# Deferred roundings, pauses in attention, and an earlier first weight split in a one-core transformer block

## The chip, the cores and the metric

The kernel runs on one core of a Trainium2 chip. The metric is the device time of one execution in microseconds (us). TensorE (PE) does the matmuls and has a separate track for weight loads (PEld); VectorE (DVE), ScalarE (ACT) and GpSimd (POOL) do the rest, and SyncE (SP), ACT and POOL issue the transfers. Each engine works through its instructions in the order in which the program lists them.

## The reference, cut to what matters

The input x has 2048 rows of 576 features. It is normalised by row, and two branches work on the result: attention with 32 heads of width 18, in which each row sees 8 keys at distances 0, 2, ... 14, and a feed-forward layer of width 4608.

```python
xn = _layernorm(x, axis=-1)
return x + _A_ref(xn, A_wqkv, A_wo) + _B_ref(xn, B_w1, B_b1, B_w2, B_b2)
```

`_A_ref` multiplies xn with wqkv, gathers 8 keys and values for each row, takes a softmax over the 8 scores and multiplies the output with wo. `_B_ref` computes `relu(xn @ w1 + b1)**2 @ w2 + b2`.

## The kernel before

**Numbers in two parts.** A float32 operand is split into a rounded part ("hi", float32r) and a remainder ("lo"). ScalarE writes the hi with an ACTIVATE Copy, and VectorE then writes the lo as a subtraction (`tt`, L95), so every lo waits for the hi of ScalarE. A product is hi·hi + lo·hi + hi·lo on TensorE.

**Tiling and phases.** The rows are four blocks `b` of 512, taken in two pairs `s`. Two matmul stages (`ffn_pair` for x·W1 and `quad_step` for x·Wqkv) use a scheme of seven products in place of eight on a pair of blocks, which needs sums of x tiles (`sums`, `last_sum`; tiles SS and S4) and sums of weight tiles (slots T1 to T4 beside B11, B21, B22). The program runs through: rows of block 0 and q, k, v for the first pair (`q0`); `phase_a(0)`, 18 steps of W1 for blocks 0 and 1 with W2 for block 0; `phase_b0`, first 36 tiles of W2 for block 1 (L493 on TensorE, squared activations read back from DRAM as `h`), then q, k, v for the second pair in four half rounds of 14 `quad_step`s (L851, L855; weight halves k = 0, 1 and row halves), then the output projection of block 1; `phase_a(1)`; `phase_b1`.

**What fills the engines meanwhile.** `phase_b0` holds a list `pieces` of generators: `normalize(2)`, `normalize(3)`, `sums(1)`, `last_sum(1)`, and the first weight slots. After each W2 tile `run(pieces, 1 + n % 2)` advances them by one or two yields, and what is left of the count goes to `side`, which advances attention. Attention of one block and one of four head groups has 18 steps: four times a product of q with shifted keys and a reduction, the softmax (its exp is on ScalarE, L361), and four times a product with shifted values and a folding sum into `q`, after which POOL writes the result to DRAM in eight transfers (`o<-q`). `release` frees a buffer of keys or values (three of them, tile `kv`), and `fetch` then issues the next load on POOL's queue. Groups of block 1 come in the order 3, 2, 1, 0. `complete(b)` runs attention until nothing of block b is left, all of it at one place in the program; it is called for block 1 by the hook at `(k, half, s, i) = (0, 1, 6, 1)`, the end of the first two half rounds, followed by `regroup(1, 0)` and the loads for block 2, all on POOL.

**The quad rounds.** In each half round two row tiles i = 0, 1 go through s = 1, 2, 3, 5, 4, 7, 6. TensorE accumulates into PSUM banks a, b, c (names p_...). After s = 1 ScalarE copies a into b (L869), and s = 3 accumulates on b. After s = 4 the row of block 3 is b + c: ScalarE copies b into the staging tile `st` (L860) and VectorE adds c (`st<-p,st`). At s = 6 TensorE accumulates on c again, so that matmul waits until VectorE has read c.

**The order.** It is the order of the program: the kernel schedules all engines by hand, and an instruction that waits holds up everything behind it on its engine.

Of the kernel before, what the change touches and what calls it, by code (L numbers as in the profile page):

```python
# [8 lines left out]
F32 = mybir.dt.float32  # L9
# [19 lines left out]
QW = 3 * CG  # L29
# [16 lines left out]
def block_kernel(ctx: ExitStack, tc: tile.TileContext, x, xt, wqkv, wo, w1, b1, w2, b2, out):  # L46
# [47 lines left out]
    def tt(out, a, b, op):  # L94
        return nc.vector.tensor_tensor(out=out, in0=a, in1=b, op=op)  # L95
# [73 lines left out]
    def load_mb(b):  # L169
        assert b in measured  # L170
        mb[b] = sb.tile([P, 2, TB], F32, name="mb")
        nc.sync.dma_start(mb[b].rearrange("c k t -> c (k t)"), flat(mrscr[b], 0, [0, P], 2 * NJ * P))

    def normalize(b):
        open_x(b)
        for a in (0, 2):
            v = xm[b][:, a:a + 2]
            for k, op in enumerate((ALU.subtract, ALU.mult)):
                tt(v, v, mb[b][:, k:k + 1].to_broadcast([P, 2, TB]), op)
                if k:  # L180
                    nc.scalar.activation(X[b][:, 0, a:a + 2], v, AF.Copy)
# [20 lines left out]
    def sums(s):  # L202
        b0, b1 = 2 * s, 2 * s + 1
        hi = lambda a: X[b0][:, 0, a:a + 2].bitcast(F32)
        lo = lambda a: X[b0][:, 1, a:a + 2].bitcast(F32)
        f, v = xm[b1][:, :2], xm[b1][:, 2:]
        e = fourth_sum[s] = four()
        for i in (1, 2, 3):
            SS[i] = mt.tile([P, 2, 2, TB], F32R, name=f"S{i}")
        low = lambda i, a: tt(SS[i][:, 1], a, SS[i][:, 0].bitcast(F32), ALU.subtract)  # L210
        high = lambda i, a: nc.scalar.activation(SS[i][:, 0], a, AF.Copy)
        tt(v, f, v, ALU.add)
        high(1, v)
# [23 lines left out]
        left_hi(x4["d"], xf[b1])  # L237
        yield
        left_lo(x4["d"], xf[b1])
        yield  # L240

# [167 lines left out]

    def run(gens, k):  # L410

        while k > 0 and gens:
# [91 lines left out]
    def ffn_pair(s, p, work, first=False):  # L504
# [245 lines left out]
    def load_left(b):  # L750
        nc.sync.dma_start(xr[b][1][:D - DM], xt[b, :D - DM, NC - 1])
# [55 lines left out]
    def split_slot(name, v):  # L807
        split(*slot(name), v)
# [2 lines left out]
        t = ws[LEFT, f] = four(F32R)[:, :, :QW]  # L811
        split(t[:, 0], t[:, 1], raw[k, "left"][:, f])

    def first_slots(k):
        v, b12 = raw[k, 0][:, 0], raw[k, 0][:, 1]
        b21, b22 = raw[k, 1][:, 0], raw[k, 1][:, 1]
        if not k:
            split_slot(B11, v)
            yield
        tt(v, b12, v, ALU.subtract)  # L820
        yield
        split_slot(T1, v)
        yield
        tt(v, b22, v, ALU.subtract)
        yield
        split_slot(T2, v)
        yield
        tt(v, b21, v, ALU.subtract)
        yield

    def third_slot(k):
        v = raw[k, 0][:, 1]
        tt(v, raw[k, 1][:, 1], v, ALU.subtract)
        split_slot(T3, v)

    QKV_BANKS = [(2, 3, 4), (5, 6, 7)]
    rows_out = [0]
# [56 lines left out]
    def phase_b0():  # L894
        b = 1
        split_up.clear()
        pieces = [normalize(2), once(load_half, 0, 0), once(load_mb, 3), normalize(3), once(load_sides, 0), sums(1),
                  once(load_half, 0, 1), once(last_sum, 1), first_slots(0), once(third_slot, 0),
                  once(split_side, 0, 0), once(split_side, 0, 1)]
        open_y(b)  # L900
        for n in range(NF):
            w2_hi()
            if n % 2 == 0:
                h_hi(0, n // 2 + 1)
            add(b, tile_products(b, n, hs[0, n // 2]), range(NC) if n == NF - 1 else ())
            w2_lo()
            if n % 2 == 0:
                h_lo(0, n // 2 + 1)
            if n % 2 and n // 2 + 3 < NP:
                load_h(0, n // 2 + 3)  # L910
            run(pieces, 1 + n % 2)
            if n == 3:
                load_xt(3)
            if n == 31:
                run_all(pieces)
            if n == 33:
                residual(b)
                xr[b].append(sb.tile([P, TB], F32, name="xf"))
                load_left(b)
            if n == 34:  # L920
                split_slot(B21, raw[0, 1][:, 0])
        for c in range(NC):
            drain(b, c)
            if c in (1, 3):
# [7 lines left out]
        def hook(k, half, s, i):  # L932
# [9 lines left out]
            if half and not k:  # L942
                if (s, i) == (1, 1):
                    split_slot(B11, raw[1, 0][:, 0])
                if (s, i) == (3, 1):
                    slots = first_slots(1)
                    for _ in slots:
                        pass
                if (s, i) == (5, 1):
                    split_slot(B21, raw[1, 1][:, 0])  # L950
                if (s, i) == (4, 1):
                    third_slot(1)
                if (s, i) == (7, 1):
                    fourth_slot(1)
                    split_side(1, 0)
                if (s, i) == (6, 1):
                    split_side(1, 1)
                    split_slot(B22, raw[1, 1][:, 1])
# [304 lines left out]
    def q0():  # L1263
# [21 lines left out]
        for r in range(len(todo) - 2):  # L1285
# [23 lines left out]
            if r == 21:  # L1309
# [86 lines left out]
```

## Time and profile before

| | |
|---|---|
| times of three runs | 1144.18, 1145.52, 1146.80 us; median 1145.52 |
| the profiled execution's own time, its span | 1146.9 us, 1145.2 us |
| PE busy | 1113.7 us, 97% |
| DVE busy | 936.2 us, 82% |
| ACT busy | 586.9 us, 51% |
| POOL busy | 116.9 us, 10% |
| mean granted TensorE clock | 0.99 |

A group's row gives the line, engine, operation, output and inputs, shapes and count, then busy time and mean ns of one, then the idle time of the engine just before it and what ended it. In a timeline the first number is the start from the span's beginning, the second the length, and the bracket holds the idle time before. In windows the engine columns are busy us with the number of instructions; PEclk is the granted clock. TensorE is busy nearly always, so what a change does is read from where it is not: the first W1 step near 96 us, the W2 tiles of `phase_b0` between 439 and 577 us, and the start of the quad rounds near 580 us.

### The profile page before, as it was taken

How to read it: one execution, taken by the hardware profiler on the slowest of the kernel's cores; microseconds unless marked ns; L12 is line 12 of the kernel's file. 1: busy time of each engine (PE TensorE's matmuls, PEld its weight loads, DVE VectorE, ACT ScalarE, POOL GpSimd, SP SyncE). 2: the span in 40 equal slices, each digit the busy share in tenths (PEclk: the TensorE clock that was granted, in tenths of full speed). 3: DMA queues.
4: the chain of work that ended last, by engine and by line, in shares of the span. 5: the costliest groups of instructions: out<-in, count | busy, mean ns of one | idle time of the engine just before them, and what ended most of it. 6: DMA issues, size and time to landing. Idle time of an engine off the chain costs nothing.

```text
span 1145.2 us, 13847 instructions
## 1 busy us (share of the span) xinstructions
PE 1113.7 (97%) x4966; PEld 932.8 (81%) x4966; DVE 936.2 (82%) x1238; ACT 586.9 (51%) x823; POOL 116.9 (10%) x219
## 2 busy tenths in 40 slices
PE   9998999999999999797989999999999999999998
PEld 7997888878888888576879988888888888888887
DVE  7696998989888987587986669898989888889864
ACT  5334665656556654335325436665566565533441
POOL 4000210202102020000102000110102020201100
PEclk9999999999999999899989999999999999999999
DMA  8953655393936376555566764635545463765672
GB/s 287 335 177 113 210 182 180 103 245 125 231 120 223 135 283 204 200 181 185 167 219 224 221 223 135 220 125 201 175 144 176 147 209 106 262 220 185 217 260 88
DMA packets 89557, 218.86 MB, mean 191 GB/s; under 512 B 12040, under 2 KB 40464, under 8 KB 83984
## 3 DMA queue, kind: packets, MB, share of 16 engines
q1 hardware_dynamic: 59456, 154.85, 40.4%
q0 software_dynamic: 10544, 52.14, 14.2%
q10 hardware_dynamic: 19488, 10.99, 3.2%
q8 instruction: 39, 0.64, 0.2%
q14 instruction: 30, 0.25, 0.1%
HBM read 174.21 MB, written 43.73 MB: 190 GB/s over the span
## 4 chain that ended last, share of the span: by engine, by line
PE 76%; DVE 13%; DMA 4%; issue 3%; ACT 3%; POOL 0%; SPq 0%; ACTq 0%; DVEq 0%; POOLq 0%
PE p L493 35%; PE p L524 26%; PE p L851 6%; PE p L528 5%; DVE pr L95 3%; DVE w1r L95 2%; DMA w2r<-in_w 2%; PE p L304 1%; DVE h L95 1%; DVE w2s L95 1%; PE p L855 1%; DVE w1s L95 1%; PE p L1180 1%; DVE lg L353 1%; DMA kvq<-st 1%
## 5 line engine op out<-in xcount | busy, mean ns | idle before, releaser
L493 PE MATMUL p<-h,w2s 128*128 128x512 f32 x2066 | 500.7, 393 | 16.0 <-ACT h L779 7.8
L493 PEld LDWEIGHTS p<-h,w2s 128*128 128x128 f32 x2066 | 389.6, 189 | 104.4 <-ACT h L779 10.3
L524 PE MATMUL p<-X,w1s 128*128 128x512 f32 x864 | 220.7, 391 | 4.5 <-DVE w1s L95 3.1
L524 PEld LDWEIGHTS p<-X,w1s 128*128 128x128 f32 x864 | 162.5, 188 | 39.3 <-DVE w1s L95 3.5
L466 ACT ACTIVATE w2s<-w2r 128x640 fp32r<-128x640 f32 x164 | 119.6, 733 | 112.4 <-PE p L493 91.3
L524 PE MATMUL p<-S,w1s 128*128 128x512 f32 x648 | 164.8, 390 | 0.0
L95 DVE TENSOR_TENSOR w2s<-w2r,w2s 128x576 fp32r<-128x576 f32 x164 | 123.5, 753 | 46.9 <-ACT w2s L466 46.5
L524 PEld LDWEIGHTS p<-S,w1s 128*128 128x128 f32 x648 | 121.9, 188 | 25.5
L381 POOL DMA_DIRECT2D o<-q x128 | 69.4, 607 | 703.1 <-DVE q L95 701.2
L95 DVE TENSOR_TENSOR w1s<-w1r,w1s 128x1024 fp32r<-128x1024 f32 (+1 forms) x78 | 94.2, 1209 | 27.0 <-ACT w1s L439 20.1
L531 ACT ACTIVATE r<-r,b1t 128x512 f32<-128x512 f32 x72 | 52.0, 723 | 111.8 <-DVE r L95 111.5
L95 DVE TENSOR_TENSOR pr<-q,kv 128x1152 f32<-128x1152 f32 x64 | 86.8, 1356 | 1.5
L95 DVE TENSOR_TENSOR pr<-lg,kv 128x1152 f32<-128x1152 f32 x64 | 86.6, 1353 | 0.8
L353 DVE TENSOR_REDUCE lg<-pr 128x64 f32<-128x1152 f32 x64 | 86.4, 1350 | 0.9
L95 DVE TENSOR_TENSOR pr<-pr 128x576 f32<-128x576 f32 (+1 forms) x128 | 77.6, 606 | 3.4
L439 ACT ACTIVATE w1s<-w1r 128x1024 fp32r<-128x1024 f32 x72 | 75.7, 1052 | 2.7 <-PE p L851 1.8
L95 DVE TENSOR_TENSOR h<-r,h 128x1024 fp32r<-128x1024 f32 (+3 forms) x46 | 51.8, 1137 | 30.8 <-ACT r L539 23.4
L539 ACT ACTIVATE r<-r 128x1024 f32<-128x1024 f32 x72 | 75.4, 1050 | 0.1
L95 DVE TENSOR_TENSOR w1r<-w1r 128x256 f32<-128x256 f32 (+3 forms) x118 | 66.1, 560 | 4.6 <-DMA w1r<-in_wqkv 2.0
L528 PE MATMUL p<-x,w1s 128*128 128x512 f32 x216 | 66.5, 389 | 0.0
L95 DVE TENSOR_TENSOR r<-p,r 128x512 f32<-128x512 f32 (+1 forms) x77 | 52.8, 686 | 9.6 <-ACT r L589 6.0
L568 ACT ACTIVATE r<-p 128x512 f32<-128x512 f32 x36 | 21.6, 600 | 68.7 <-PE p L524 68.7
(169 smaller groups left out, 1111.7 us busy)
## 6 DMA issues: line engine op xcount, KB each, us to landing
w2r<-in_w SPq DMA_DIRECT2D x144, 320.0 KB, 3.1
kv<-kvq POOLq DMA_DIRECT2D x29, 1296.0 KB, 7.0
w1r<-in_w SPq DMA_DIRECT2D x36, 640.0 KB, 4.9
h<-r SPq DMA_DIRECT2D x36, 512.0 KB, 3.3
h<-h SPq DMA_DIRECT2D x36, 512.0 KB, 4.1
kvq<-st ACTq DMA_DIRECT2D x48, 216.0 KB, 2.8
w2r<-in_wo SPq DMA_DIRECT2D x20, 320.0 KB, 3.0
w1r<-in_xt SPq DMA_DIRECT2D x6, 1024.0 KB, 6.8
```

What stands on the lines that cost most here:

```text
L95: return nc.vector.tensor_tensor(out=out, in0=a, in1=b, op=op)
L353: nc.vector.tensor_reduce(out=lg[:, j * HG:(j + 1) * HG].rearrange("p a w -> p w a"), in_=pr.rearrange("p w (a d) -> p w a d", d=DH), axis ...
L381: nc.gpsimd.dma_start(rows[:, i], q[i * L:(i + 1) * L, :, a:z])
L439: nc.scalar.activation(w1s[n, k][:, 0], raw1[n][:, 4 * k:4 * k + 4], AF.Copy)
L466: nc.scalar.activation(w2s[stream[i]][:, :DE], raw2[i], AF.Copy)
L493: nc.tensor.matmul(yp[b][c], v, a, start=c not in yb[b], stop=c in last and c not in [o[0] for o in ops[i + 1:]], skip_group_check=True)
L524: nc.tensor.matmul(to, l, r, start=start and i == 0, stop=i == len(mm) - 1, skip_group_check=True)
L528: nc.tensor.matmul(to, weight(LEFT, k, f), v, start=False, stop=k == 1, skip_group_check=True)
L531: nc.scalar.activation(to, a, AF.Relu, bias=b1t[:, f:f + 1])
L539: nc.scalar.activation(r, r, AF.Square)
L568: nc.scalar.activation(u[:, 0], bb, AF.Copy)
L851: nc.tensor.matmul(to, l[:, js], r, start=start and n == 0, stop=n == len(mm) - 1, skip_group_check=True)
```

## The change

1. `soon(f)` and `flush()`: with `defer[0]` set, a hi is put in a list in place of being issued; it is issued at the next `flush()`, which stands at the start of every `run()` and ahead of a lo. `defer` is set for the part of `phase_b0` up to n = 33.
2. In `phase_b0` the pieces have rests in them (`rest(4)` between the two normalisations, `rest(2)` ahead of the slots; each yield makes one attention step), the transfer of block 3's mean and scale (`load_mb(3)`) goes ahead of `load_half`, `last_sum` and the slots are cut into more yields (hi in one, lo in a later one), and T3 and the side slots are now in the same generator. `run` stops at n < 33, and what is left runs at n = 33 in place of 31.
3. The slots of the second weight half are spread over the second half round: hi at one hook, lo at a later one.
4. In `ffn_pair` the attention steps for s = 0 go from 3 to `2 + p % 2`.
5. In `q0` the first W1 tile is split at rows 23 and 24 in place of 24 and 25, and row 22 runs no piece.

```diff
+    later, defer = [], [False]
+    def soon(f):
+        if defer[0]:
+            later.append(f)
+        else:
+            f()
+    def flush():
+        while later:
+            later.pop(0)()
...
     def normalize(b):
...
-                    nc.scalar.activation(X[b][:, 0, a:a + 2], v, AF.Copy)
+                    soon(lambda v=v, a=a: nc.scalar.activation(X[b][:, 0, a:a + 2], v, AF.Copy))
...
-        left_hi(x4[b], xf[b])
+        soon(lambda: left_hi(x4[b], xf[b]))
         yield
         for a in (0, 2):
+            flush()
             tt(X[b][:, 1, a:a + 2], xm[b][:, a:a + 2], X[b][:, 0, a:a + 2].bitcast(F32), ALU.subtract)
...
     def sums(s):
...
-        low = lambda i, a: tt(SS[i][:, 1], a, SS[i][:, 0].bitcast(F32), ALU.subtract)
-        high = lambda i, a: nc.scalar.activation(SS[i][:, 0], a, AF.Copy)
+        def low(i, a):
+            flush()
+            tt(SS[i][:, 1], a, SS[i][:, 0].bitcast(F32), ALU.subtract)
+        high = lambda i, a: soon(lambda: nc.scalar.activation(SS[i][:, 0], a, AF.Copy))
...
     def run(gens, k):
+        flush()
...
     def ffn_pair(s, p, work, first=False):
...
-            side(1 if p == 1 else 2 + p % 2 if s else 3, False)
+            side(1 if p == 1 else 2 + p % 2, False)
...
+    def rest(k):
+        for _ in range(k):
+            side(1)
             yield
...
     def phase_b0():
...
-        pieces = [normalize(2), once(load_half, 0, 0), once(load_mb, 3), normalize(3), once(load_sides, 0), sums(1),
-                  once(load_half, 0, 1), once(last_sum, 1), first_slots(0), once(third_slot, 0),
-                  once(split_side, 0, 0), once(split_side, 0, 1)]
+        defer[0] = True
+        pieces = [normalize(2), once(load_mb, 3), once(load_half, 0, 0), rest(4), normalize(3), once(load_sides, 0),
+                  sums(1), once(load_half, 0, 1), last_sum_parts(1), rest(2), first_slots()]
...
-            run(pieces, 1 + n % 2)
+            if n < 33:
+                run(pieces, 1 + n % 2)
...
-            if n == 31:
+            if n == 33:
                 run_all(pieces)
-            if n == 33:
+                defer[0] = False
                 residual(b)
...
             if half and not k:
                 if (s, i) == (1, 1):
-                    split_slot(B11, raw[1, 0][:, 0])
+                    slot(B11)
+                    slot_hi(B11, v)
+                if (s, i) == (2, 0):
+                    slot_lo(B11, v)
...
-            if r in (24, 25):
-                w1_hi(0, r - 24)
-                w1_lo(0, r - 24)
-            elif r != 3:
+            if r in (23, 24):
+                w1_hi(0, r - 23)
+                w1_lo(0, r - 23)
+            elif r not in (3, 22):
                 run(pieces, 3 if r < 1 or 15 <= r < 20 else 1 if r > 20 else 2)
```

TensorE's order is the same in both programs, and no engine has more or fewer instructions in all. What moves is on VectorE and ScalarE, at three places.

**VectorE at the end of the first two half rounds** (k = 0), where `complete(1)` stands. Bank c of row tile 0 is p_4658 before and p_4592 in the change. Before:

```order
L95 TENSOR_TENSOR r_4967<-mb,r_4967 128x432
L95 TENSOR_TENSOR st<-p_4670,st 128x432
L95 TENSOR_TENSOR r_4981<-mb,r_4981 128x432
L95 TENSOR_TENSOR h<-w1r,h 128x2x432
L95 TENSOR_TENSOR pr<-q,kv 128x1152
L353 TENSOR_REDUCE lg<-pr 128x8x8
L95 TENSOR_TENSOR pr<-q,kv 128x1152
L353 TENSOR_REDUCE lg<-pr 128x8x8
L95 TENSOR_TENSOR st<-p_4658,st 128x432
```

In the change, from the same weight slot (B22's lo, `h<-w1r,h`) on:

```order
L95 TENSOR_TENSOR r_4911<-mb,r_4911 128x432
L95 TENSOR_TENSOR h<-w1r,h 128x2x432
L95 TENSOR_TENSOR pr<-pr 128x576
L95 TENSOR_TENSOR pr<-pr 128x288
L95 TENSOR_TENSOR q<-pr 128x144
L95 TENSOR_TENSOR pr<-lg,kv 128x1152
```

and, with 32 rows between, its end:

```order
L95 TENSOR_TENSOR pr<-lg,kv 128x1152
L95 TENSOR_TENSOR pr<-pr 128x576
L95 TENSOR_TENSOR pr<-pr 128x288
L95 TENSOR_TENSOR q<-pr 128x144
L95 TENSOR_TENSOR pr<-q,kv 128x1152
L372 TENSOR_REDUCE lg<-pr 128x8x8
L95 TENSOR_TENSOR pr<-q,kv 128x1152
L372 TENSOR_REDUCE lg<-pr 128x8x8
L95 TENSOR_TENSOR st<-p_4592,st 128x432
```

Before, block 2's first attention steps follow the slot at once. In the change 40 rows of block 1's attention stand between them: the last three folding sums of group 1 with the two value products between them, and all of group 0 (four query products and reductions, the softmax, four value products and folding sums).

**ScalarE at the same place**, from B22's hi on (L869 is L920 in the change, L874 is L925, L361 is L380). Before:

```order
L99 ACTIVATE r_4981<-mb 128x432
L99 ACTIVATE h<-w1r 128x2x432
L869 ACTIVATE p_4657<-p_4656 128x432
L869 ACTIVATE p_4668<-p_4667 128x432
L874 ACTIVATE p_4659<-p_4657 128x432
```

In the change:

```order
L99 ACTIVATE r_4911<-mb 128x432
L99 ACTIVATE h<-w1r 128x2x432
L380 ACTIVATE lg<-lg 128x256
L920 ACTIVATE p_4591<-p_4590 128x432
L920 ACTIVATE p_4602<-p_4601 128x432
L925 ACTIVATE p_4593<-p_4591 128x432
```

The exp of group 0 now stands ahead of the copies of a into b for the next half round.

**ScalarE in the first W2 tiles of `phase_b0`**, with the hi of block 2's x (X, L181 before, L193 in the change; `w2s<-w2r` is the hi of a W2 tile, L466 and L486). Before:

```order
L466 ACTIVATE w2s<-w2r 128x640
L181 ACTIVATE X_3768<-w1r 128x1024
L466 ACTIVATE w2s<-w2r 128x640
L779 ACTIVATE h<-h 128x1024
L181 ACTIVATE X_3768<-w1r 128x1024
L466 ACTIVATE w2s<-w2r 128x640
L195 ACTIVATE x_3769<-xf 128x512
```

In the change:

```order
L486 ACTIVATE w2s<-w2r 128x640 x2
L799 ACTIVATE h<-h 128x1024
L193 ACTIVATE X_3724<-w1r 128x1024
L486 ACTIVATE w2s<-w2r 128x640
L193 ACTIVATE X_3724<-w1r 128x1024
L209 ACTIVATE x_3725<-xf 128x512
```

A hi of x now stands behind the hi of the next W2 tile, where it stood ahead of it.

More of the change, by code (lines that the diff above doesn't have):

```diff
@@ L410, in run @@
     def run(gens, k):
+        flush()
         while k > 0 and gens:
@@ L812, in split_side, with slot_hi, slot_lo, last_sum_parts @@
         split(t[:, 0], t[:, 1], raw[k, "left"][:, f])
[L814 to L818, printed above, removed]
+    def slot_hi(name, v):
+        soon(lambda: nc.scalar.activation(ws[name][0], v, AF.Copy))
+    def slot_lo(name, v):
+        flush()
+        tt(ws[name][1], v, ws[name][0].bitcast(F32), ALU.subtract)
+    def rest(k):
+        for _ in range(k):
+            side(1)
             yield
-        tt(v, b12, v, ALU.subtract)
+    def last_sum_parts(s):
+        b, e = 2 * s + 1, fourth_sum[s]
+        soon(lambda: nc.scalar.activation(X[b][:, 0, :2], e, AF.Copy))
         yield
-        split_slot(T1, v)
+        flush()
+        tt(X[b][:, 1, :2], e, X[b][:, 0, :2].bitcast(F32), ALU.subtract)
+        yield
+    def first_slots():
+        v, w, b21, b22 = raw[0, 0][:, 0], raw[0, 0][:, 1], raw[0, 1][:, 0], raw[0, 1][:, 1]
+        for name in (B11, T1, T2, T3):
+            slot(name)
+        slot_hi(B11, v)
+        yield
+        slot_lo(B11, v)
+        yield
+        tt(v, w, v, ALU.subtract)
+        slot_hi(T1, v)
+        yield
+        tt(w, b22, w, ALU.subtract)
+        slot_hi(T3, w)
+        yield
+        slot_lo(T1, v)
         yield
         tt(v, b22, v, ALU.subtract)
+        slot_hi(T2, v)
         yield
-        split_slot(T2, v)
+        slot_lo(T3, w)
+        yield
+        slot_lo(T2, v)
         yield
         tt(v, b21, v, ALU.subtract)
+        for f in range(2):
+            ws[LEFT, f] = four(F32R)[:, :, :QW]
+            soon(lambda f=f: nc.scalar.activation(ws[LEFT, f][:, 0], raw[0, "left"][:, f], AF.Copy))
         yield
[L831 to L834, printed above, removed]
+        for f in range(2):
+            flush()
+            tt(ws[LEFT, f][:, 1], raw[0, "left"][:, f], ws[LEFT, f][:, 0].bitcast(F32), ALU.subtract)
+            yield
     QKV_BANKS = [(2, 3, 4), (5, 6, 7)]
@@ L919, in phase_b0 @@
                 load_left(b)
+                slot(B21)
+                slot_hi(B21, raw[0, 1][:, 0])
             if n == 34:
-                split_slot(B21, raw[0, 1][:, 0])
+                slot_lo(B21, raw[0, 1][:, 0])
         for c in range(NC):
@@ L957, in hook @@
                     split_side(1, 1)
-                    split_slot(B22, raw[1, 1][:, 1])
+                    split_slot(B22, b22)
                     complete(1)
```

31 lines of the change are left out of this document (25 added, 6 removed).

## The prediction

> **What bounds the kernel now.** I read the page first, then TensorE's waits, then the windows and timelines around them.
>
> ```profile
> PE 76%; DVE 13%; DMA 4%; issue 3%; ACT 3%; POOL 0%; SPq 0%; ACTq 0%; DVEq 0%; POOLq 0%
> ```
>
> TensorE is the bound (the chain that ended last is three quarters PE), and its work does not change. So the change can win only what TensorE now waits, and lose what it will wait. TensorE's waits by engine and line (total, times, longest, us):
>
> ```profile
> PE p L493 <- ACT h L779: 7.8, 6, 3.1
> PE p L493 <- DVE w2s L95: 5.8, 1, 5.8
> PE p L851 <- DVE h L759: 4.9, 1, 4.9
> PE p L524 <- DVE w1s L95: 3.1, 1, 3.1
> ```
>
> The first two are the W2 tiles of `phase_b0`, the third the first quad rounds, the last the first W1 step. The whole of the W2 stage (504 matmuls, 439 to 577 us) stands in one group: its idle time is 15.7 us. A long wait also lowers the granted clock behind it (window: PE busy and count; then the other engines; then the clock):
>
> ```profile
> L493 PE MATMUL p<-h,w2s 128*128 128x512 f32 x504 | 122.1, 402 | 15.7 <-ACT h L779 7.8 <-DVE w2s L95 5.8 <-ACT w2s L466 2.0
> 470.00:480.00 10.00, 7.82 (x22) 6.22 (x23) 7.29 (x7) 2.35 (x3) 0.00 (x0) 0.66 0.32 97
> 540.00:550.00 10.00, 6.85 (x24) 5.32 (x23) 9.31 (x16) 4.93 (x7) 0.00 (x0) 0.83 0.33 109
> 560.00:570.00 10.00, 10.00 (x46) 8.27 (x45) 9.86 (x12) 3.29 (x4) 4.35 (x8) 1.00 0.61 182
> 580.00:590.00 10.00, 6.95 (x25) 6.51 (x26) 8.67 (x14) 2.18 (x4) 0.00 (x0) 0.66 0.53 167
> 630.00:640.00 10.00, 10.00 (x53) 9.60 (x52) 8.64 (x9) 3.18 (x6) 0.54 (x1) 1.00 1.03 337
> ```
>
> At full clock 10 us hold 46 W2 matmuls or 53 quad matmuls. So 22 in 7.82 us of busy time lost 7.82 − 4.78 = 3.0 us, 24 in 6.85 lost 1.6, and 25 in 6.95 lost 2.2: a mean of 2.3 us for each wait of 3 to 6 us.
>
> **The change, part by part: what it wins.** In the W2 stage the big wait has a transfer behind it, and the small ones a rounding ahead of a W2 tile's:
>
> ```profile
> 470.23 1.23 DVE L95 TENSOR_TENSOR w1r<-w1r,mb 128x1024 f32<-128x1024 f32 x1 [7.71 <-DMA mb<-mr]
> 474.43 1.06 ACT L181 ACTIVATE X<-w1r 128x1024 fp32r<-128x1024 f32 x1 [13.49 <-DVE w1r L95]
> 476.14 0.76 DVE L95 TENSOR_TENSOR w2s<-w2r,w2s 128x576 fp32r<-128x576 f32 x1 [1.75 <-ACT w2s L466]
> ```
>
> VectorE waited 7.71 us for block 3's mean and scale. Four rests put its use about three tiles later, 3 · 14 / 4.6 = 9.1 us, and the transfer is issued ahead of two others: this wait goes. The last rows show the ping-pong: the remainder of the W2 tile waits 1.75 us since ScalarE rounds x first, which itself waits for VectorE. With x rounded behind the next W2 tile that goes too. What can be won is 15.7 + 3.0 + 1.6 = 20.3 us. Against it: in the first 21 tiles VectorE has, by these durations, 21 · 0.76 of W2 remainders, 11 · 1.22 of `h`, and 38 us of normalisation, sums and rests (22 operations of 1.22, 8 of half that width, by estimate 0.7 each, and rests of two value products with their sums, 6.0), 67 us together, where TensorE needs 21 · 3.04 = 64. So it runs level with TensorE, and something may still be late: I leave 2 us (bounds 0 and 12) and count 18.3. Behind it VectorE has room, since attention has left this stage: in the 560 to 570 window it was 99% busy and TensorE ran through.
>
> At the start of the quad rounds TensorE waited 4.92 us for the drains of the finished banks, which stood behind attention on VectorE; now two rows of W2 stand there. I count 4.9 + 2.2 − 0.5 = 6.6 us (bounds 4 and 7).
>
> In the first W1 step TensorE waited 3.1 us for the first remainder:
>
> ```profile
> 89.24 1.60 DVE L95 TENSOR_TENSOR w1r<-w1r 128x512 f32<-128x512 f32 x3
> 95.29 2.35 DVE L95 TENSOR_TENSOR w1s<-w1r,w1s 128x1024 fp32r<-128x1024 f32 x2
> ```
>
> One value product and its folding sum (3.0 us below) leave the way, and the hi is issued a row sooner, right behind the combination that ends at 90.84: the win is 2.9 us (bounds 2 and 4). The fewer steps in `phase_a(0)` cost nothing there, since TensorE does not wait in it; what they put off is counted next. Together 18.3 + 6.6 + 2.9 = 27.8 us.
>
> **What it loses.** Attention steps are not saved but put off: 8 in `phase_a(0)` (one for each even p from 2 to 16), 1 in `q0`, and by the counts of yields about 12 in the W2 stage. What is left falls due at `complete(1)`, as 40 VectorE rows in one piece. Their prices, from the same steps elsewhere in this stage:
>
> ```profile
> 579.59 0.41 DVE L359 TENSOR_REDUCE mx<-lg 128x32 f32<-128x256 f32 x1
> ...
> 582.25 2.73 DVE L759 SCALAR_TENSOR_TENSOR h<-p,b2t,h 128x512 f32<-128x512 f32 x4
> ...
> 587.97 1.35 DVE L95 TENSOR_TENSOR pr<-lg,kv 128x1152 f32<-128x1152 f32 x1
> 589.35 1.25 DVE L95 TENSOR_TENSOR pr<-pr 128x576 f32<-128x576 f32 x2
> 590.64 0.31 DVE L95 TENSOR_TENSOR q<-pr 128x144 f32<-128x144 f32 x1
> 590.98 1.36 DVE L95 TENSOR_TENSOR pr<-lg,kv 128x1152 f32<-128x1152 f32 x1
> ...
> 604.75 0.31 DVE L95 TENSOR_TENSOR q<-pr 128x144 f32<-128x144 f32 x1
> ...
> 627.92 1.05 DVE L95 TENSOR_TENSOR h<-w1r,h 128x864 fp32r<-128x864 f32 x1
> 628.89 1.35 DVE L95 TENSOR_TENSOR pr<-q,kv 128x1152 f32<-128x1152 f32 x1
> ...
> 631.67 1.36 DVE L95 TENSOR_TENSOR pr<-q,kv 128x1152 f32<-128x1152 f32 x1
> ...
> 634.39 0.61 DVE L95 TENSOR_TENSOR st<-p,st 128x432 f32<-128x432 f32 x1
> ```
>
> A value product with its sum takes 590.98 − 587.97 = 3.01 us, the sum alone 1.6, a query product with its reduction 631.67 − 628.89 = 2.78, the softmax 582.25 − 579.59 = 2.66. The piece is 1.6 + 2 · 3.01 + 4 · 2.78 + 2.66 + 4 · 3.01 = 33.4 us. On the clock of before it starts at 628.97, where B22's remainder ends, and ends at 662.4.
>
> Behind it stand four steps of block 2's attention, which need a new load of keys. POOL issues that load only after the result of the last group and its regrouping:
>
> ```profile
> 605.35 4.32 POOL L381 DMA_DIRECT2D o<-q  x8 [38.77 <-DVE q L95]
> 609.72 0.56 POOL L693 DMA_DIRECT2D kv<-o  x1
> 611.46 0.54 POOL L693 DMA_DIRECT2D kv<-o  x1 [1.18 <-DMA o<-q]
> 619.99 0.54 POOL L324 DMA_DIRECT2D q<-kvq  x1 [7.99 <-DMA kvq<-st]
> kv<-kvq POOLq DMA_DIRECT2D x29, 1296.0 KB, 7.0
> 638.30 1.32 PE L851 MATMUL p<-h,X 128*128 128x432 f32 x6
> ```
>
> Before, this queue ran at 605, with over 20 us to spare. From the last `q` (604.75 + 0.31) to the end of the regrouping's issue (612.00) are 6.9 us; the queries' issue is 0.5, the keys land 7.0 after theirs: 14.4 us. So the keys are there at 662.4 + 14.4 = 676.8. Then come the four steps, 634.39 − 628.89 = 5.5, and `st<-p` for bank c, 0.6: 682.9. TensorE wants bank c at 638.30 (its s = 6). It waits 44.6 us, of which about 21 pass earlier, at s = 3: the exp stands ahead of the copies on ScalarE and cannot start before 628.97 + 7.6 + 11.1 + 0.9 = 648.6. That part is inside the 44.6, not added. With 2.3 us of low clock after it, the loss is 46.9 us. Bounds: 30.2 + 2.3 if the keys did not hold (the 33.4 alone, 668.5 − 638.30), and 49 if the load takes 2 us more. I take the long chain, since each step of it has its row. Two low-clock spells cost no more than one, as the first lies in the second wait.
>
> The Trainium skill (TensorE: Matmul & The Clock Gate, section "What's actually happening") says that TensorE falls to half clock after an idle window of about 3.4 us and comes back after a busy one of the same length. By that the restart would cost an estimated 1.7 us and the loss 46.3; the windows above, with 0.66 after 5.8 and 4.9 us and 1.00 around the waits of 1 us, agree in kind. The Trainium skill (DMA: Bandwidth & Descriptors, section "Anatomy of one DMA — SWDGE (gpsimd) path") prices a transfer at 2.0 us plus its bytes at 436 GB/s, an estimated 5.0 us for the keys, which would make the loss 2 us smaller; the row of 7.0 is from this kernel with other traffic beside it.
>
> **The sum.** 46.9 − 27.8 = +19.1 us, on the span of 1145.2 gives 1164.3. The profiled execution took 1146.9, so 1166.0 like it; against the median of 1145.5 the same step gives 1164.6.
>
> **The rivals.** *VectorE stays the bound in the W2 stage*: the 67 against 64 us bring new small waits, and only 8 of 20.3 us are won. For it: VectorE level with TensorE. Against: at 99% busy it held TensorE up nowhere. 1164.6 + 10 = 1175. *The keys come in time*, so that only the 33.4 us count: −14.4, 1150. It needs POOL free of the last group's result, which its order speaks against. *The piece is hidden and the kernel is faster*: TensorE would have to find bank c read less than 25.5 us late (27.8 − 2.3), so the keys in time and 5 of the 33.4 us done before B22's remainder. With this and nothing left at c it ends at 1143, and at 1118 if nothing waited. Against: the piece has one place in the program, and no engine steps over a waiting row. *The deferral does nothing*: the roundings wait elsewhere, only 9.5 us are won, and the time is 1145.5 + 46.9 − 9.5 = 1183. Against: ScalarE is half idle, and the order shows each hi behind the W2 tile's.
>
> **How the numbers follow.** Forecast 0.68, VectorE bound 0.13, keys in time 0.08, hidden 0.05, deferral idle 0.06. The forecast's own bounds are 1157 to 1174. I widen to 1149 and 1178, which takes in the second and third and leaves out the last two and some of the tails. A change under 0.2%, 2.3 us, cannot be told from none here. Faster: 0.06, the hidden case and a tail. Same: 0.03. Slower: 0.91.
>
> **What would show it.** Right: between 439 and 577 TensorE's idle time falls from 15.7 to a few us and the clock stays at 1.00; the wait at L851 on the drain is gone; there are two new waits at the quad matmuls, some 20 us on ScalarE's copies of a into b and then over 20 us on `st`, in the third half round; VectorE has a run of over 30 us of attention without a gap, then a gap of about 14 us that a transfer of keys ends. Wrong: no such gap (keys in time), or the W2 stage still idle by 10 us. The likeliest error of size is the wait for the keys, 14.4 us, and the 2 us left in the W2 stage.

## The result, and the profile after

The changed kernel takes 1156.49 us (median; 1156.03 to 1157.82), the kernel before 1145.15 us beside it: a ratio of 1.0099, 95% interval 1.0082 to 1.0117. It is slower, by 11 us where 19 were forecast. The profiled spans are 1156.1 and 1145.2 us.

Line numbers shift: L493, L524, L466, L851, L860, L869, L759 and L779 of before are L513, L544, L486, L902, L911, L920, L779 and L799 after. The chain of work that ended last, by engine, and TensorE's waits (total, times, longest, us), of the changed kernel:

```profile
PE 91%; DVE 5%; DMA 1%; issue 1%; ACT 1%; POOL 0%; ACTq 0%; POOLq 0%; DVEq 0%
...
PE p L902 <- DVE st L95: 23.6, 1, 23.6
PE p L902 <- ACT p L920: 19.9, 1, 19.9
...
PE p L544 <- DVE w1s L95: 0.4, 1, 0.4
PE p L513 <- ACT h L555: 0.2, 1, 0.2
```

The waits of before in the W2 tiles and at the drains are gone, and the one in the first W1 step is down from 3.1 to 0.4 us. Two new ones have come, in the third half round. TensorE's timeline of the changed kernel (start, length, operation, and in the bracket the idle time before it):

```profile
433.10 114.70 PE L513 MATMUL p<-h,w2s 128*128 128x512 f32 x504
547.64 2.51 PE L902 MATMUL p<-r,X 128*128 128x432 f32 x12
...
567.22 2.48 PE L902 MATMUL p<-r,X 128*128 128x432 f32 x12
...
586.76 2.48 PE L902 MATMUL p<-r,X 128*128 128x432 f32 x12
589.08 2.50 PE L902 MATMUL p<-w1s,S 128*128 128x432 f32 x12
611.48 3.91 PE L902 MATMUL p<-w1s,S 128*128 128x432 f32 x12 [19.89 <-ACT p L920]
...
646.81 2.53 PE L902 MATMUL p<-h,X 128*128 128x432 f32 x6 [23.59 <-DVE st L95]
...
653.94 2.48 PE L902 MATMUL p<-r,X 128*128 128x432 f32 x12
```

The 504 products of the W2 stage stand in one unbroken row of 114.70 us, where before they were 122.1 us with 15.7 us of idle time. The third half round starts at 586.76 and ends at 653.94. On VectorE, ScalarE and POOL of the changed kernel stands why:

```profile
590.88 1.25 DVE L95 TENSOR_TENSOR pr<-pr 128x576 f32<-128x576 f32 x2
...
624.08 0.31 DVE L95 TENSOR_TENSOR q<-pr 128x144 f32<-128x144 f32 x1
640.71 1.36 DVE L95 TENSOR_TENSOR pr<-q,kv 128x1152 f32<-128x1152 f32 x1 [16.32 <-DMA kv<-kvq]
...
646.16 0.60 DVE L95 TENSOR_TENSOR st<-p,st 128x432 f32<-128x432 f32 x1
```

```profile
610.59 0.42 ACT L380 ACTIVATE lg<-lg 128x256 f32<-128x256 f32 x1 [21.10 <-DVE lg L95]
610.91 0.93 ACT L920 ACTIVATE p<-p 128x432 f32<-128x432 f32 x2
```

```profile
624.68 4.31 POOL L400 DMA_DIRECT2D o<-q  x8 [21.54 <-DVE q L95]
...
631.84 0.54 POOL L345 DMA_DIRECT2D kv<-kvq  x1
```

The piece of attention runs on VectorE from 590.88 to 624.39 without a gap, 33.5 us. The exp inside it stands ahead of ScalarE's copies of a into b (L920): TensorE's first wait ends with them. VectorE then stands for 16.32 us before keys that POOL could issue only behind the last `q`. Four steps later comes the `st<-p` row that TensorE's second wait is for.

By stages, from the starts of TensorE's rows in both timelines (us):

| stage | before | after | gain | forecast |
|---|---|---|---|---|
| up to the first W2 product (first W1 step) | 117.71 | 113.72 | 4.0 | 2.9 |
| `phase_a(0)`, to the W2 stage of block 1 | 321.4 | 319.4 | 2.0 | 0 |
| W2 stage, 504 products | 137.7 | 114.5 | 23.1 | 18.3 |
| first half round (drains ahead of it) | 26.8 | 19.6 | 7.2 | 6.6 |
| second half round | 19.6 | 19.5 | 0.1 | 0 |
| third half round | 19.7 | 67.2 | −47.4 | −46.9 |
| fourth half round, and the rest | 502.2 | 502.2 | 0 | 0 |

The gains sum to 36.4 us, the loss is 47.4: 11.0 us, which is the difference of the spans, 10.9.

### The profile page after: what moved, and what is told of

Its sections match the earlier page's. It is cut to its first block, busy times and chain, and to the rows that moved or that the text cites. A ratio compares the mean times of both kernels' runs of the same rounds, so it can differ in the third digit from the quotient of the medians.

```text
span 1156.1 us, 13845 instructions
## 1 busy us (share of the span) xinstructions
PE 1105.7 (96%) x4966; PEld 931.0 (81%) x4966; DVE 938.3 (81%) x1238; ACT 588.2 (51%) x823; POOL 117.5 (10%) x219
## 4 chain that ended last, share of the span: by engine, by line
PE 91%; DVE 5%; DMA 1%; issue 1%; ACT 1%; POOL 0%; ACTq 0%; POOLq 0%; DVEq 0%
PE p L513 45%; PE p L544 29%; PE p L548 5%; PE p L323 5%; PE p L902 5%; DVE pr L95 2%; PE p L1253 1%; PE p L906 1%; DMA kv<-kvq 1%; DVE lg L372 1%; DMA kv<-in_x 0%; DVE w1s L95 0%; POOL o L400 0%; DVE r L95 0%; PE p L1215 0%
## 5 line engine op out<-in xcount | busy, mean ns | idle before, releaser
L513 PE MATMUL p<-h,w2s 128*128 128x512 f32 x2066 | 493.2, 390 | 0.3 <-ACT h L555 0.2
L513 PEld LDWEIGHTS p<-h,w2s 128*128 128x128 f32 x2066 | 387.2, 188 | 83.6 <-ACT h L555 1.0
L544 PE MATMUL p<-X,w1s 128*128 128x512 f32 x864 | 219.5, 389 | 0.4 <-DVE w1s L95 0.4
L544 PEld LDWEIGHTS p<-X,w1s 128*128 128x128 f32 x864 | 162.1, 188 | 34.3 <-DVE w1s L95 0.8
L486 ACT ACTIVATE w2s<-w2r 128x640 fp32r<-128x640 f32 x164 | 120.5, 735 | 128.4 <-PE p L513 97.9
L544 PE MATMUL p<-S,w1s 128*128 128x512 f32 x648 | 164.5, 389 | 0.0
L544 PEld LDWEIGHTS p<-S,w1s 128*128 128x128 f32 x648 | 121.6, 188 | 25.3
L95 DVE TENSOR_TENSOR pr<-q,kv 128x1152 f32<-128x1152 f32 x64 | 86.8, 1357 | 17.9 <-DMA kv<-kvq 16.3
L588 ACT ACTIVATE r<-p 128x512 f32<-128x512 f32 x36 | 21.6, 599 | 71.2 <-PE p L544 71.2
```

The lines of the kernel that those rows point to most:

```text
L486: nc.scalar.activation(w2s[stream[i]][:, :DE], raw2[i], AF.Copy)
L513: nc.tensor.matmul(yp[b][c], v, a, start=c not in yb[b], stop=c in last and c not in [o[0] for o in ops[i + 1:]], skip_group_check=True)
L544: nc.tensor.matmul(to, l, r, start=start and i == 0, stop=i == len(mm) - 1, skip_group_check=True)
```

## The experiments

All edits are on the changed kernel, but for e; the diffs of g and l are shown against f and k. Ratios are to the kernel before, run beside it, with 95% intervals.

**a: the number of attention steps in `phase_a(0)` put back.**

```diff
-            side(1 if p == 1 else 2 + p % 2, False)
+            side(1 if p == 1 else 2 + p % 2 if s else 3, False)
```

> The change with its fourth edit undone (three attention steps for s = 0 again). Theory (the loss is the attention that falls due in one piece at complete(1), and the keys' load queued behind it): the piece shrinks to the end of the softmax and four value products, 1.2 + 4 * 3.01 = 13.3 us in place of 33.4, and the exp leaves it, so the wait of 19.9 us on ScalarE's copies goes and the wait on st is the key chain alone; phase_a(0) is 2 us longer. 1156.5 - 20.1 + 2.0 = 1138.4. Rival (the length of the piece does not decide, the keys or the order on ScalarE do): 1150 or more. Rival (the steps taken out of phase_a(0) are what gave the 6 us there): phase_a(0) 6 us longer, 1142.

Measured: 1137.91 us, 0.9936 [0.9915, 0.9958]. The piece has shrunk to the softmax's tail and four value products, 13.3 us, the wait on L920 is gone, and the third half round takes 46.4 us in place of 67.2. So the piece's length sets a part of the loss one to one: 20.1 us less piece, 20.8 us less time. `phase_a(0)` itself takes 320.7 us here, 1.3 us more than in the changed kernel.

**b: no deferral.**

```diff
-        defer[0] = True
+        defer[0] = False
```

> The change with the roundings issued at once (the list is never used), all rests and the earlier transfer kept. Theory (the deferral removes the small waits, the rests and the earlier transfer the one long wait): the W2 stage gets back the waits on ScalarE of before, 9.9 us idle and some 2 us of low clock, 114.5 to about 126 us, and the loss at the quad rounds stays: 1166 to 1169. Rival (the rests and the lighter load of attention won the whole stage, the deferral nothing): 1156.5.

Measured: 1165.49 us, 1.0176 [1.016, 1.0191]. The group of W2 products in b, in the window of its stage:

```profile
L513 PE MATMUL p<-h,w2s 128*128 128x512 f32 x504 | 117.1, 392 | 5.0 <-ACT h L799 4.2 <-ACT w2s L486 0.6
```

The waits on ScalarE are back: 5.0 us idle and 117.1 − 114.7 = 2.4 us more of busy time, 7.4 together, where some 12 were expected. The rival "the deferral does nothing" falls. But the deferral is a third of the 23.1 us; the other two thirds come from what else the change did to this stage.

**c: no attention steps in the third half round.**

```diff
-                    if (s, i) in (...) and (k, half) != (0, 1):
+                    if (s, i) in (...) and (k, half) not in ((0, 1), (1, 0)):
```

> The change without the attention steps of the third half round, so that the bank's read no longer stands behind steps that need the new keys. Theory: the wait for the keys (16.3 us) and the four steps (5.4 us) leave the way, the piece of 33.4 us stays, with the wait of 19.9 us on ScalarE: 1156.5 - 21.5 = 1135, up to 1138 if the keys hold the fourth half round. Rival (the piece on VectorE alone sets the end of the wait, the keys arrive within it): no change, 1156.5. Rival (the eight steps put off come back as a new piece in phase_a(1)): 1146 or more.

Measured: 1144.86 us, 0.9991 [0.9982, 1.0001], some 10 us above what was expected. The third half round did what it should: 43.0 us in place of 67.2, so the keys' wait and the four steps behind it are 24.2 us of the loss. But the fourth takes 25.3 us in place of 19.5, and the rest 489.2 in place of 482.6. In the fourth it is the keys again, as VectorE's timeline of c shows: the wait for them has moved there and is shorter.

```profile
641.83 1.36 DVE L95 TENSOR_TENSOR pr<-q,kv 128x1152 f32<-128x1152 f32 x1 [8.99 <-DMA kv<-kvq]
```

That the longer rest is the steps that were left out, coming back later, is argued here and not shown. The rival "come back as a new piece" had 1146 or more, and the time lies between the two.

**d: a and c together.**

> Both: three steps for s = 0 and no attention in the third half round. Theory: the piece of 13.3 us ends about 2 us after TensorE wants the bank, and the keys hold the fourth half round for about 3 us, so of the 47.4 us some 5 are left, and phase_a(0) is 2 us longer: 1156.5 - 47.4 + 7 = 1116. Rival (the two parts overlap and only one of them can be had): 1135. Rival (steps put off cost it later): 1125 or more.

Measured: 1126.54 us, 0.9833 [0.9818, 0.9849], again some 10 us above: the time is that of the rival "steps put off cost it later" (1125 or more). TensorE's and VectorE's timelines of d:

```profile
587.06 2.48 PE L902 MATMUL p<-r,X 128*128 128x432 f32 x12
...
605.29 1.69 PE L902 MATMUL p<-h,X 128*128 128x432 f32 x6 [3.23 <-DVE st L95]
...
611.65 2.48 PE L902 MATMUL p<-r,X 128*128 128x432 f32 x12
```

```profile
621.40 1.36 DVE L95 TENSOR_TENSOR pr<-q,kv 128x1152 f32<-128x1152 f32 x1 [6.86 <-DMA kv<-kvq]
```

The third half round takes 24.6 us. So the loss comes apart into two parts that nearly add: with the long piece 67.2 us with the keys' wait and 43.0 without it, with the short one 46.4 and 24.6. The keys cost 24.2 or 21.8 us, the 20 us of piece 20.8 or 18.4. What stays open in d is 4.9 us here (the 13.3 us of piece), 3.4 in the fourth half round, where VectorE still stands for keys at 621.40, and 6.2 in the rest.

**e: the earlier W1 split alone, on the kernel before.**

```diff
-            if r in (24, 25):
+            if r in (23, 24):
...
-            elif r != 3:
+            elif r not in (3, 22):
```

> The kernel before with only the last part of the change: the first W1 tile is split at rows 23 and 24 instead of 24 and 25, and row 22 issues no pieces. My theory takes the first W1 step as a term by itself: the changed kernel starts the first W2 product at 113.72 us against 117.71 us, so 4.0 us should come through to the end and nothing else should move: 1141 us (1140 to 1142). A rival says that the step only hands its wait on, because the W2 stage of block 1 is bound by VectorE and the later stages have slack of their own: then the first W2 product starts sooner and the end stays at 1145 us.

Measured: 1142.06 us, 0.9952 [0.9939, 0.9964]; the span is 3.8 us shorter. The first W2 product starts at 113.69, 4.0 us sooner. The win comes through; it is not handed on.

**f: the piece laid out over the third half round.** `complete(1)`, `regroup` and the offers move from the hook (0, 1, 6, 1) to (1, 0, 6, 1); a's edit is in it.

```diff
-                    complete(1)
...
+            if at == (1, 0, 6, 1):
+                complete(1)
...
-                    if (s, i) in (...) and (k, half) != (0, 1):
+                    if (s, i) in (...) and (k, half) != (0, 1) and ((k, half) != (1, 1) or s == 7 or (s, i) == (4, 1)):
```

> The changed kernel with three steps per pair of tiles in phase_a(0) as before, and the attention that is left at the end of the second half round laid out step by step over the third, eight steps, with complete(1), the gather and the offers at its end; in the fourth half round three steps, after the keys can have landed. If the piece of rows on VectorE is what the third half round waits for, and the keys what the fourth waits for, both now take some 19.7 us each: the rest of the program starts near 627 us, and with 482.7 to 490 us behind it (some steps come back later, as they did in the run without third-round steps) the end is 1110 to 1120 us. If instead the keys' landing decides in any order, or the st rows are late whatever VectorE does first, the two half rounds keep some 8 us of wait and the end is 1124 to 1130 us.

Measured: 1135.8 us, 0.9903 [0.9884, 0.9921]. The third and the fourth half rounds take 19.5 us each without a wait, as the first theory has it. The end is 16 us beyond it: the rest takes 505.6 us, 23 more than in the changed kernel. Its two largest waits, one of TensorE's waits and one row of its timeline of f:

```profile
PE p L513 <- DVE w2s L95: 10.8, 1, 10.8
...
632.74 0.79 PE L513 MATMUL p<-h,w2s 128*128 128x512 f32 x1 [4.83 <-ACT st L911]
```

The first is a second piece. `complete(3)`, at tile 22 of `phase_b1`, finds attention left (five steps fewer than in d were done in the half rounds), and a W2 tile's remainder waits behind it. The second stands at the start of the output projection, where ScalarE's copy into `st` is late; its own timeline has it wait 4.48 us for the transfers of finished rows (`kvq<-st`). Why these took so long was not tried.

**g: f, with two steps per tile in the first twelve tiles of `phase_b1`.**

```diff
-            side(1 + n % 2)
+            side(2 if n < 12 else 1 + n % 2)
```

> The same as f, and two steps per tile instead of one or two in the first twelve tiles of the last W2 stage, so that six put-off steps are made up there where VectorE has room. If the time lost behind 635 us in c and d is put-off attention that makes the gather of block 3 late, this gives 482.7 to 485 us behind the half rounds: 1108 to 1113 us, some 3 to 7 us less than f. If that loss has another cause (the rows of the output projection alone), it is within 1 us of f.

Measured: 1133.08 us, 0.9877 [0.9862, 0.9892], with 504.4 us of rest. The medians differ by 2.7 us, but the intervals of f and g overlap and the spans differ by 1.1: at most a small win. The one wait of 10.8 us has become six on W2 remainders, 6.6 us together, and those on ScalarE's `h` have grown from 1.5 to 2.8 us: VectorE has no room there for six more steps. Put-off attention is paid for in this stage, in one piece or in many.

**h: no rests.**

```diff
-        pieces = [normalize(2), once(load_mb, 3), once(load_half, 0, 0), rest(4), normalize(3), ...
-                  sums(1), once(load_half, 0, 1), last_sum_parts(1), rest(2), first_slots()]
+        pieces = [normalize(2), once(load_mb, 3), once(load_half, 0, 0), normalize(3), ...
+                  sums(1), once(load_half, 0, 1), last_sum_parts(1), first_slots()]
```

> The changed kernel without rest(4) and rest(2) in the list of pieces of the W2 stage of block 1, so that the pieces follow each other without the tiles in between that only run attention steps. If the rests are what lets loads and sums arrive, waits come back in this stage (114.5 us now, up to 118) and the end is 1157 to 1161 us; if the deferral and the order alone carry the gain, the stage stays at 114.5 to 115 us and the end at 1155 to 1158 us, give or take what six attention steps more or less change in the later piece (1.4 us each).

Measured: 1160.3 us, 1.011 [1.0094, 1.0126]; the W2 stage takes 118.8 us, 4.2 more. VectorE's and TensorE's timelines of h:

```profile
460.08 1.23 DVE L95 TENSOR_TENSOR w1r<-w1r,mb 128x1024 f32<-128x1024 f32 x1 [6.62 <-DMA mb<-mr]
```

```profile
462.03 89.80 PE L513 MATMUL p<-h,w2s 128*128 128x512 f32 x388 [2.37 <-DVE w2s L95]
```

It is the big wait of the kernel before, for block 3's mean and scale. TensorE loses less by it here (2.37 us idle, where it was 5.84), so something else in the change has shortened it; the earlier issue of the transfer was not tried alone. The rests remove what is left of it, as the prediction had it.

**i: attention brought forward.** The deferral stays, and nothing is put off: more steps ahead of the half rounds, softmax allowed in the first, and in the third only the last four steps.

```diff
-            side(1 if p == 1 else 2 + p % 2, False)
+            side(1 if p == 1 else 2 + p % 2 if s else 4 if p > 9 else 3, False)
...
+                if n > 21 and n % 2 == 0:
+                    side(1)
...
-                    if (s, i) in (...) and (k, half) != (0, 1):
-                        side(1, s == 7)
+                    if (s, i) in (...) and (k, half) != (0, 1) and ((k, half) != (1, 0) or s > 3 and (s, i) != (5, 0)):
+                        side(1, s == 7 or not (k or half))
```

> The changed kernel with the attention of block 1 brought forward instead of put off: three steps per pair in phase_a(0) and four from the tenth pair on, one step more in every other of the last twelve tiles of the W2 stage, softmax allowed in the whole first half round, so that complete(1) finds nothing left; and in the third half round steps only from its ninth quad step on. If put-off attention is what the half rounds and the rest of the program pay for, no piece is left before the keys' gather, which goes out near 588 us; keys land by some 599 us, the third and fourth half rounds take 19.6 to 21 us each, the rest 483 to 486 us: end at 1110 to 1116 us. If VectorE has no room in the stages before, their waits come back: W2 stage 116 to 122 us instead of 114.5, end at 1116 to 1125 us.

Measured: 1124.21 us, 0.9816 [0.9796, 0.9835]. The half rounds behave (19.6 us each) and the rest takes 484.0 us. But `phase_a(0)` has no room for a fourth step, as TensorE's waits of i show:

```profile
PE p L544 <- DVE r L95: 7.1, 7, 1.4
```

The W2 stage starts at 442.02 in place of 433.90 in a. The stage itself still takes 114.5 us, with the added steps in it. Another 3.8 us go in the first half round, 23.4 us in place of 19.6: the drains wait for a transfer, as VectorE's timeline of i shows.

```profile
559.09 2.73 DVE L779 SCALAR_TENSOR_TENSOR h<-p,b2t,h 128x512 f32<-128x512 f32 x4 [3.98 <-DMA h<-in_xt]
```

**j: i without the fourth step.** Three steps in `phase_a(0)`; the rest of the diff is as in i.

> The same as i without the fourth step per pair in phase_a(0): at complete(1) three steps are left (a piece of some 4.5 us instead of none). Where the third half round is paid for by the length of the piece, it takes 0 to 3 us more than in i, since the rows can wait 1.4 us per quad step; the rest as in i: 1111 to 1119 us. If it is the keys' landing that counts, it is later by the 4.5 us.

Measured: 1127.94 us, 0.9845 [0.9826, 0.9864]. The third half round takes 30.9 us. VectorE's timeline of j shows that it is the keys:

```profile
599.69 0.31 DVE L95 TENSOR_TENSOR q<-pr 128x144 f32<-128x144 f32 x1
602.17 0.61 DVE L95 TENSOR_TENSOR st<-p,st 128x432 f32<-128x432 f32 x1 [2.18 <-ACT st L911]
617.22 1.36 DVE L95 TENSOR_TENSOR pr<-q,kv 128x1152 f32<-128x1152 f32 x1 [14.44 <-DMA kv<-kvq]
```

From the last `q` to the keys' use pass 617.22 − 600.00 = 17.2 us; a step that asks for them sooner holds every `st` row behind it. Here TensorE waited 9.8 us. The first half round takes 22.3 us, again with the drains behind `h<-in_xt`.

**k: the short piece, and no steps in the third half round.** Three steps in `phase_a(0)`, the added steps of the W2 stage at tiles 22 to 29 only, five steps in the second half round, none in the third.

```diff
-                    if (s, i) in (...) and (k, half) != (0, 1):
-                        side(1, s == 7)
-                    if (s, i) in ((2, 1), (5, 0), (7, 0)) and (k, half) == (0, 1):
+                    if (s, i) in (...) and (k, half) != (0, 1) and ((k, half) != (1, 0)):
+                        side(1, s == 7 or not (k or half))
+                    if (s, i) in ((2, 1), (5, 0), (4, 1), (7, 0), (7, 1)) and (k, half) == (0, 1):
```

> The run d (three steps per pair in phase_a(0), none in the third half round) with a shorter piece: one step more in every other of the tiles 22 to 29 of the W2 stage, softmax allowed in the whole first half round, five steps instead of three in the second. At complete(1) the sums of one value product and one whole product are left, some 4.7 us instead of d's 13.3 us. If the piece's length sets what the third half round waits for, it takes 19.6 to 20.5 us instead of d's 24.6 us; keys go out some 9 us sooner, so the fourth takes 19.6 to 21 us instead of 22.9 us, and behind it the rest is 483 to 488 us instead of 488.9 us, as the steps of the fourth run on time: 1113 to 1119 us. If the put-off steps come back whatever the keys do, the rest stays at 489 us or more and the end at 1119 to 1124 us.

Measured: 1120.68 us, 0.9779 [0.9758, 0.98]. The third half round takes 19.5 us, the fourth 21.6, the rest 489.6. A piece of 4.7 us is hidden whole. The rest is where the second reading of the expectation had it (489 us or more, the end at 1119 to 1124), not the first. Of the 7.0 us that it takes more than in the changed kernel, 5.5 lie where the output projection begins, at the late `st` rows. TensorE's timeline of k:

```profile
630.61 0.49 PE L513 MATMUL p<-h,w2s 128*128 128x512 f32 x1 [0.56 <-ACT st L911]
632.04 0.50 PE L513 MATMUL p<-h,w2s 128*128 128x512 f32 x1 [0.93 <-DVE st L95]
633.90 11.43 PE L513 MATMUL p<-h,w2s 128*128 128x512 f32 x38 [1.37 <-DVE st L95]
```

**l: k without the last two steps of the fourth half round.**

```diff
-                    if (s, i) in (...) and (k, half) != (0, 1) and ((k, half) != (1, 0)):
+                    if (s, i) in (...) and (k, half) != (0, 1) and (k, half) != (1, 0) and (k, half, s) != (1, 1, 7):
```

> The run k without the last two attention steps of the fourth half round, whose rows were late on VectorE when the output projection began (waits of 0.56, 0.93 and 1.37 us and 2.5 us of low clock in k). If these two steps are what makes the rows late, the fourth half round takes 20 to 21 us and the waits behind it go; two steps come back later at 1.4 us each, which the rest of the program hides or not: 1112 to 1117 us. If put-off steps cost more where they come back than where they are left out, as between c, d and f, the end is 1119 to 1126 us.

Measured: 1116.09 us (1115.33 to 1118.19), 0.9738 [0.9721, 0.9755], the fastest of all. The rest falls from 489.6 to 485.0 us, and TensorE is busy nearly throughout. The page and TensorE's timeline of l:

```profile
PE 1104.0 (99%) x4966; PEld 927.1 (83%) x4966; DVE 933.9 (84%) x1238; ACT 588.1 (53%) x823; POOL 116.7 (10%) x219
```

```profile
588.59 2.48 PE L902 MATMUL p<-r,X 128*128 128x432 f32 x12
...
608.13 2.48 PE L902 MATMUL p<-r,X 128*128 128x432 f32 x12
...
630.72 9.63 PE L513 MATMUL p<-h,w2s 128*128 128x512 f32 x40 [0.57 <-ACT st L911]
```

The half rounds and the rest, from the starts of the TensorE rows (us). In b, e and h the edits are elsewhere; the third half round takes 66.7 us in b, 19.7 in e and 65.3 in h:

| | before | after | a | c | d | f | g | i | j | k | l |
|---|---|---|---|---|---|---|---|---|---|---|---|
| third half round | 19.7 | 67.2 | 46.4 | 43.0 | 24.6 | 19.5 | 19.5 | 19.6 | 30.9 | 19.5 | 19.5 |
| fourth | 19.6 | 19.5 | 19.6 | 25.3 | 22.9 | 19.5 | 19.5 | 19.6 | 20.2 | 21.6 | 21.4 |
| rest | 482.7 | 482.6 | 482.8 | 489.2 | 488.9 | 505.6 | 504.4 | 484.0 | 482.6 | 489.6 | 485.0 |

## Why the prediction was right, and where it was off

The measured 1156.5 us lies in the stated range of 1149 to 1178, but half a microsecond below the sum's own bounds, 1157 to 1174.

**The loss** was right in place and mechanism: 47.4 us against 46.9. The piece is 33.5 us (33.4 forecast). Bank c is read late for the reason given. The piece and the keys nearly add, as c, a and d show, so the rival "the keys in time" (1150) falls, and so does "the piece is hidden". From the last `q` to the keys' use it took 16.3 us, not 14.4, 1.9 us more. That the sum comes out within 0.5 us is partly luck: the forecast took the start of the piece from the clock of before, 628.97 − 623.23 = 5.7 us into the third half round, and in the changed kernel it starts 590.88 − 586.76 = 4.1 us into it, which takes 1.6 us back. TensorE is slow behind both new waits, as forecast: twelve products in 3.91 us at 611.48 against 2.50, and six in 2.53 us at 646.81 against 1.35.

**The win was mis-sized**, and that is the part that failed: 36.4 us in place of 27.8. These 8.6 us, less the 0.5 by which the loss was larger, are the whole distance between 1164.6 and 1156.5.

- *W2 stage*, 23.1 in place of 18.3. "I leave 2 us" was not needed: the row of 504 has no wait in it, though VectorE was forecast to run level with TensorE. And "what can be won" was 15.7 + 7.4 = 23.1, not 20.3 us. The row of before says 122.1 us busy, the row after 114.7 us: 7.4 us of its busy time was lost too, of which the two windows had given 3.0 + 1.6 for slow matmuls. Of the other 2.8 us some 1.7 are, by estimate, the ten breaks in the row of before: a product that stands alone reads 0.40 us long (f at 627.51), and one within the unbroken row takes 114.70 / 504 = 0.23, so each break adds 0.17. The rest lies behind the smaller waits. The group's own busy time against 504 matmuls at full clock would have given it.
- *What carries it*: the deferral 7.4 us (b), the rests 4.2 us (h), as far as taking each away alone shows. The remaining 11.5 us were not taken apart; the earlier transfer, the finer pieces and their new order, and the attention steps that left this stage are all in them. The fewer steps in `phase_a(0)` are not: in a, which undoes them, the stage takes 114.5 us as well.
- *First W1 step*, 4.0 in place of 2.9: the wait fell from 3.06 to 0.35 us, and the slow matmuls behind it, which the term left out, are the rest. It stands alone (e).
- *`phase_a(0)`*, 2.0 in place of 0. "TensorE does not wait in it" is wrong. TensorE's waits of before have a line for it, and its timeline has the two waits:

```profile
PE p L524 <- DVE r L95: 1.4, 2, 1.2
...
252.68 1.65 PE L524 MATMUL p<-X,w1s 128*128 128x512 f32 x6 [1.16 <-DVE r L95]
...
270.95 1.66 PE L524 MATMUL p<-X,w1s 128*128 128x512 f32 x6 [0.28 <-DVE r L95]
```

  With the two breaks and the six products behind each that take 1.65 in place of 1.52 us, they come to the 2.0 us. These waits stand in every kernel with three steps (0.3 us in d to 1.8 in j, and the phase takes 320.3 to 321.8 us) and in none with the fewer ones (the changed kernel, b, c and h, 319.3 to 319.4 us). So the fewer steps are what won it, and a shows it by itself: there the waits are back, 0.7 us, with 1.3 us more of phase.
- *Drains*, 7.2 in place of 6.6: a little above its bound of 7.

"VectorE stays the bound in the W2 stage" falls with the unbroken row; "the deferral does nothing" falls with b.

**My expectations for c, d, f, g and i** were off on one side, by 7 to 20 us. Each took it that a wait removed is time won. But attention steps are a fixed amount of VectorE work (it is busy for 936.2 us before, 938.3 after and 933.9 in l), and the steps that used to run beside the waits had to run elsewhere: at `complete(3)` (f, g), in `phase_a(0)` (i) and, as far as the late `st` rows tell, at the output projection (c, d, k). In c and d the wait for the keys also moved on into the fourth half round. In j, 9 us above its range, the step that asks for keys was put too early, against the 17 us that they take. k came out 2 us above its first reading, within its second, and l within its first, once steps were taken out where a row of the timeline had shown TensorE waiting for VectorE.

## What to carry to other kernels

Work that is put off on an engine that works in order falls due in one place: before taking steps out of a stage, find the place that completes them, and price there the length of the piece and the transfer that can start only behind it. Both parts add, and here they turned a change that wins 36 us into one that loses 11; with the same roundings and splits, and the steps kept early or left out of the rounds in which TensorE waited for them, the kernel is 2.6% faster than before (l). What a stage can win is its whole time less its matmuls at full clock; listed idle time alone leaves out the slow matmuls behind each wait, and the end of the row at each break.

## What the runs showed of the hardware that was not expected

The same short waits cost 2.5 us in one run and nothing in another. At the start of the output projection k and d wait almost alike; 38 products then take 11.43 us in k (above), and in d, by its TensorE timeline:

```profile
635.80 0.51 PE L513 MATMUL p<-h,w2s 128*128 128x512 f32 x1 [0.58 <-ACT st L911]
637.22 0.49 PE L513 MATMUL p<-h,w2s 128*128 128x512 f32 x1 [0.91 <-DVE st L95]
639.08 8.90 PE L513 MATMUL p<-h,w2s 128*128 128x512 f32 x38 [1.37 <-DVE st L95]
```

The granted clock was 0.75 in k from 630 to 635 us and 0.57 from 635 to 640; in d it was 1.00 throughout from 625 to 650. None of these waits is longer than 1.4 us, but between them TensorE did single products. The Trainium skill (TensorE: Matmul & The Clock Gate, section "What's actually happening") says that the clock follows the activity in a free-running window of about 3.4 us, so that it depends on where in the window the work falls. The pair of rows agrees with that; no run here shows the window itself.

The keys' load also took longer than its median. In the changed kernel VectorE got its keys 640.71 − 631.84 = 8.9 us after POOL began to issue them, where the page's median to landing is 7.1.
